# Moving the second pair's key rotation on GpSimd to the start of the kernel, and the last tokens' small copies to ScalarE

## The chip, the cores and the metric

The kernel runs on one NeuronCore of one Trainium2 chip. The metric is device time in microseconds (us) of one execution; lower is better. Five engines work side by side, each through its own instructions in order: TensorE (PE in the profile, with its weight loads as PEld), VectorE (DVE), ScalarE (ACT), GpSimd (POOL) and SyncE (SP), which here only issues transfers.

## The reference

Attention with rotary embedding over 2 batches of 8 heads (576 tokens, head size 64), then a dense feed-forward layer with softplus, then a mixture of eight experts of which each token takes one. Only the attention is touched here:

```python
def rotate(x):
    x1, x2 = (x[..., :half], x[..., half:])
    return np.concatenate([x1 * cos - x2 * sin, x1 * sin + x2 * cos], axis=-1)
q_rot, k_rot = (rotate(q), rotate(k))
scale = 1.0 / np.sqrt(D)
scores = scale * np.matmul(q_rot, k_rot.transpose(0, 1, 3, 2))
scores = scores - np.max(scores, axis=-1, keepdims=True)
attn = np.exp(scores)
attn = attn / (np.sum(attn, axis=-1, keepdims=True) + 1e-09)
return np.matmul(attn, v)
# then x = softplus(x @ w_in) @ w_out, and x = gate * relu(x @ w1[e]) @ w2[e] for each token's expert e
```

## The kernel before, in words

The 16 heads are worked on in 8 pairs (m = 0 to 7). Of each head's 576 tokens the first 512 lie as 128 partitions times 4, and the last 64 (the "tails") are handled apart. Numbers are kept exact by splitting each operand into a rounded high part and the rest, the low part.

For a pair, the raw keys and queries are rotated (`rotary`, L273: four elementwise instructions at L264, two multiplications of 128x512 by the cosines and sines, one subtraction and one addition of 128x256), turned by four TensorE transposes (`turn`, L311) and split: ScalarE copies the high part from PSUM (L341), VectorE subtracts it to give the low part (L359 for keys, L363 for queries). Both halves of the 128 partitions need copies, so `kqt` (L322) sends four transfers for a pair's keys (two after the high part, two after the low part) and six for its queries (four after the high part, two after the low part), all on SP's queue (L335, L365).

The first pair is on a path of its own (L1348 to L1365 and the steps for s up to 3): VectorE rotates its heads one after the other in 128x256 and 128x128 pieces (`first_rotary`, L410), `again` (L426) copies the rotated head beside itself, and the turns follow (`first_keys`, `first_queries`, `first_tails`). `first_tails` gives three steps: `more`, `second` (eight small copies for the first pair, L485) and `third` (seven small copies for the second pair, L495). `pcopy` (L67) is a copy on GpSimd, `acopy` (L70) one on ScalarE.

A loop over slots s then runs the scores: pair m = s // 9, block i = s % 9. A slot has the matmuls of one block (L526, `scores`), the row maximum on VectorE (L543) and the exponential on ScalarE (L544) one slot later; the PSUM banks of the scores alternate, so the matmuls of slot s wait for the exponential of slot s - 2. Work for coming pairs is put into the slots by hand: `later(n, f)` runs f at the end of the n-th slot from now, `tick` runs what is due. In slot 5 the second pair's queries are turned and split, in slot 6 its keys, and slot 9 is the second pair's first block. `warm(n)` adds n matmuls that feed nothing. The schedule is manual: each engine takes its instructions in program order.

Of the kernel before, what the change touches and what calls it, by code (L numbers as in the profile page):

```python
# [20 lines left out]
def kernel(  # L21
# [32 lines left out]
    NPR = NH // 2  # L54
# [12 lines left out]
    def pcopy(o, i):  # L67
        nc.gpsimd.tensor_scalar(out=o, in0=i, scalar1=1.0, scalar2=0.0, op0=ALU.mult, op1=ALU.add)  # L68

    def acopy(o, i):  # L70
        nc.scalar.activation(out=o, in_=i, func=ACTF.Copy)  # L71
# [145 lines left out]
    up, dn = slice(0, 64), slice(64, 128)  # L217
    xraw, rot, vst, kq, prob, stat, unit, xps, rsb, tls = ({} for _ in range(10))
# [54 lines left out]
    def rotary(m, nm, engs, ts=None):  # L273
        r = r_r[nm].next()
        rot[m, nm] = r
        out = r.rearrange("p (j h t d) -> p h j t d", j=4, h=2, t=2)
        return rotate(xraw.pop((m, nm)), False, *(ts or (r_t1.next(), r_t2.next())), out, engs)

    def rotary_tails(engs, c0=0):

        rot["t"] = x_tl
        x, t1, t2 = x_tl[:, c0:], r_t1.next()[:, c0:], r_t2.next()[:, c0:]
        return rotate(x, True, t1, t2, x.rearrange("p (g j t d) -> p g j t d", g=1, t=2, d=32), engs)
# [142 lines left out]
    def again(r, hs=slice(0, 2), copy=acopy):  # L426
        copy(r[:, :, hs, 1], r[:, :, hs, 0])
# [38 lines left out]
    def first_tails():  # L466

        tp = tbank()
        turn(tp, [rot["t0"][:, c, h].rearrange("p u d -> p (u d)") for c in range(2) for h in range(2)])
        hi, lo = r_u.bufs[2][:, 0:512], r_u.bufs[2][:, 512:1024]  # L470
        v = lambda a: a.rearrange("p (c h t s) -> p c h t s", c=2, h=2, t=2)
        hv, lv, tv = v(hi.bitcast(F32)), v(lo.bitcast(F32)), v(tp)
        st, w, _ = kq[0, "xk"]
        acopy(hi[:, 0:256], tp[:, 0:256])
        acopy(st[up, :, 576:640], tv[up, 0, :, 0])
        vsub(st[dn, :, 576:640], tv[dn, 0, :, 0], hv[dn, 0, :, 0])
        qs = tl_q[0][:, 0:512].rearrange("p (c h s) -> p c h s", c=2, h=2)
        ql = tl_ql[0][:, 0:256].rearrange("p (c h s) -> p c h s", c=2, h=2)

        def more():  # L480
            acopy(hi[:, 256:512], tp[:, 256:512])
            acopy(w[up, 576:640], tv[up, 0, 0, 0])
            later(1, lambda: vsub(lo, tp, hi.bitcast(F32)))

        def second():  # L485
            pcopy(w[dn, 576:640], hv[dn, 0, 1, 0])
            for h in range(2):
                pcopy(qs[:, :, h, 64 * h:64 * h + 64], hv[:, :, h, 1])
            pcopy(ql[up, :, 0], lv[up, :, 0, 1])
            pcopy(ql[dn, :, 1], lv[dn, :, 1, 1])  # L490
            pcopy(st[up, 1, 0:64], hv[up, 0, 1, 0])
            pcopy(st[dn, 1, 0:64], lv[dn, 0, 1, 0])
            pcopy(w[:, 0:64], hv[:, 0, 1, 0])

        def third():  # L495
            st, w, _ = kq[1, "xk"]
            for r, a in ((up, hv), (dn, lv)):
                pcopy(st[r, :, 576:640], a[r, 1, :, 0])
                pcopy(st[r, 1, 0:64], a[r, 1, 1, 0])
            pcopy(w[up, 576:640], hv[up, 1, 0, 0])  # L500
            pcopy(w[dn, 576:640], hv[dn, 1, 1, 0])
            pcopy(w[:, 0:64], hv[:, 1, 1, 0])

        return more, second, third

# [841 lines left out]
    vec, pool = nc.vector, nc.gpsimd  # L1347
# [6 lines left out]
    k_high()  # L1354
    q_high, q_low = first_queries(0)
    warm(4)
    again(rot["t0"])
    q_high()
    k_low()
    q_low()  # L1360
    t_more, t_second, t_third = first_tails()
    for f in first_rotary("xk", 1, vec, 4):
        f()
    again(rot[0, "xk"], slice(1, 2), pcopy)
    warm(3)  # L1365
    nc.vector.tensor_copy(tids, tokens.rearrange("p (t a) -> p t a", a=2))
    nc.scalar.dma_start(out=taut, in_=tau.rearrange("(a b) -> a b", a=1).to_broadcast([128, 1]))
# [4 lines left out]
    for s in range(NSL + 17):  # L1372
        m, i = divmod(s, 9)
        ma = m - 1 if 4 <= i <= 8 else m - 2
        add = None

        if hl:
            hl[0]()
        if ex:
            ex()  # L1380
        ending = 0 <= ma < NPR and i in (3, 8)
        if ending:
            add = fin(ma, i == 3)
        if hl:
            hl[1]()
        if hlt:
            hlt[0]()
        begin()
        ex = scores(m, i) if s < NSL else None
        if hlt:  # L1390
            hlt[1]()

        extra = None
        if i == (2 if m else 6) and m + 1 < NPR:
            extra = kqt(m + 1, "xk")
        if i == 5 and m + 1 < NPR:
            extra = kqt(m + 1, "xq")
        if i == 6 and 1 <= m <= NPR:
            extra = inv[2]()
        if i == 7 and m < NPR:  # L1400
            extra = tails(m)
        if i == 3 and 1 <= m <= NPR:
            extra = tails4(m - 1)
        if s == 8:
            extra = kqt_tails(0, 2)
        if s == 28:
            extra = kqt_tails(1)
        if s in (65, NSL + 7):
            extra = x_tails(0 if s == 65 else 1)
        if extra:  # L1410
            extra[0]()
        if add:
            add()
        if ending and i == 3:
            for n, f in enumerate(finish(ma)):
                later(n + 2, f)
        if extra:
            extra[1]()

        mt = m - 1 if i == 8 else None  # L1420
        if s >= NSL:
            mt = NPR - 1 if s == NSL + 5 else None
        hlt = av_tails(mt) if mt is not None and mt >= 0 else None
        if i and 0 <= ma < NPR:
            for u in AVS.get(i, ()):
                av(ma, u)

        mt, it = divmod(s - 10, 9)
        hl = transp(mt, UB[it]) if 0 <= mt < NPR else None
        if i == 0 and 0 <= ma < NPR:  # L1430
            for u in AVS.get(i, ()):
                av(ma, u)

        if s in UNPACK:
            unpack(True)
        if s >= FF:
            if s > FF and (s - FF) % 2 == 0:
                ffn1_act(*u_done)
                unpack(True)
            if (s - FF) % 2 == 0:  # L1440
                u_done = units.pop(0)
            ffn1_mm(*u_done, range(2 * ((s - FF) % 2), 2 * ((s - FF) % 2) + 2))
        if i == 5 and m < NPR:
            recip(m, slice(8, 9))
        if i == 0 and 1 <= m <= NPR:
            inv = inverse(m - 1)
            later(1, inv[0])
            later(2, inv[1])
        if i == 4 and m + 2 < NPR:
            for n, f in enumerate(rotary(m + 2, "xk", nc.gpsimd)):  # L1450
                later(n, f)
        if i == 8 and m + 2 < NPR:
            for n, f in enumerate(rotary(m + 2, "xq", nc.gpsimd)):
                later(n, f)
        if i == 8 and m + 3 < NPR:
            load(m + 3, "xk")
        if i == 4 and m and m + 2 < NPR:
            load(m + 2, "xq")
        if i == 1 and 1 <= m < NPR:
            load(m, "xv")  # L1460
        if i == 4 and m < NPR:
            for n, f in enumerate(vsplit(m)):
                later(n, f)
        if s == 5:
            for n, f in enumerate(vsplit_tails()):
                later(n, f)
        if s == 15:
            load_tails(1)

        if s == 21:  # L1470
            for f in rotary_tails(nc.gpsimd):
                f()
        if s == 46:
            for n, f in enumerate(vsplit_tails()):
                later(n, f)
        if s == 0:
            k_high, k_low = first_keys(1)
            k_high()
            t_more()
            later(1, t_second)  # L1480
        if s == 1:
            k_low()
            for f in first_rotary("xq", 1, vec, 6):
                f()
            again(rot[0, "xq"], slice(1, 2))
        if s == 2:
            for f in rotary(1, "xk", pool):
                f()
            q_high, q_low = first_queries(1)
            q_high()  # L1490
            for n, f in enumerate(rotary(1, "xq", nc.vector, (r_pp.bufs[5][:, 0:512], r_pp.bufs[5][:, 512:1024]))):
                later(min(n, 2), f)
            load(2, "xk")
            load(2, "xq")
        if s == 3:
            q_low()
        if s == 4:
            for f in rotary_tails(nc.gpsimd, 256):
                f()
        if s == 6:  # L1500
            t_third()
            for b in range(2):
                nc.gpsimd.memset(y_tl[b], 0.0)
        if s < 10:
            warm(2)
        tick()
        if s == NSL - 12:
            for _ in range(3):
                fetch()
# [339 lines left out]
```

## Time and profile before

| what | value |
|---|---|
| median of 3 runs | 532.79 us (531.74 to 533.05) |
| the profiled execution | 530.74 us |
| its span, first to last instruction | 529.0 us |
| TensorE matmuls busy | 505.5 us (96% of the span) |
| VectorE, ScalarE, GpSimd busy | 349.5, 312.7, 286.3 us |
| mean granted TensorE clock | 0.992 of full speed |

The rows count in microseconds from the span's start. In the timeline a row begins with start and duration; "x4" is four merged instructions, whose duration runs from the first start to the last end; the bracket gives idle time just before on that engine and what ended it. `fa` holds raw and rotated queries and keys, `g` scratch and probabilities, `rm` and `xd` the split operands, `pp` is PSUM.

### The profile page before, as it was taken

The numbers are of one execution on the slowest core, as the hardware profiler recorded it, in microseconds if no ns is written. First come the engines' busy times: TensorE is split into PE (matmuls) and PEld (weight loads), VectorE is DVE, ScalarE is ACT, GpSimd is POOL, SyncE is SP. The second block draws the span as 40 slices with busy tenths as digits, with TensorE's granted clock in tenths as the row PEclk, the third lists the DMA queues.
The fourth block names the chain that finished last, engine by engine and source line by source line (L and its number), as shares of the span: only waits on it lengthen the run. The fifth ranks groups of instructions, "written<-read, shape, count | busy, mean of one in ns | idle before, by whom it ended". The sixth has DMA issues, their size and how long they took to land. (4 is left out here: it accounts for less than half of the span.)

```text
span 529.0 us, 9306 instructions
## 1 busy us (share of the span) xinstructions
PE 505.5 (96%) x3184; PEld 449.8 (85%) x3184; DVE 349.5 (66%) x766; ACT 312.7 (59%) x662; POOL 286.3 (54%) x308
## 2 busy tenths in 40 slices
PE   7779999999989999999999999999999999999995
PEld 6578888889878989999998888888888989898794
DVE  7768888878899689999896222367647347156220
ACT  5569999999987666446966333345443255245321
POOL 1697889787436556654448445566775525300001
PEclk9889999999999999999999999999999999999999
DMA  7156656544643234444330000522221467600000
GB/s 177 39 136 173 163 125 163 150 115 114 152 148 91 80 120 151 156 144 159 124 114 2 14 28 21 145 69 86 61 105 43 150 257 241 212 10 21 20 6 34
DMA packets 45096, 57.09 MB, mean 108 GB/s; under 512 B 17112, under 2 KB 31448, under 8 KB 45040
## 3 DMA queue, kind: packets, MB, share of 16 engines
q1 hardware_dynamic: 41904, 48.76, 31.9%
q0 software_dynamic: 2704, 7.25, 4.0%
q8 instruction: 27, 0.44, 0.3%
q10 hardware_dynamic: 432, 0.41, 0.3%
q14 instruction: 29, 0.24, 0.1%
HBM read 40.17 MB, written 5.16 MB: 86 GB/s over the span
## 5 line engine op out<-in xcount | busy, mean ns | idle before, releaser
L803 PE MATMUL pp<-xb,rm 128*128 128x288 f32 x768 | 107.1, 298 | 1.8 <-POOL rm L68 1.0
L803 PEld LDWEIGHTS pp<-xb,rm 128*128 128x128 f32 x768 | 103.0, 189 | 4.4 <-DVE g L820 1.8
L845 PE MATMUL pp<-rm,parts 128*128 128x512 f32 x432 | 105.2, 397 | 0.0
L845 PEld LDWEIGHTS pp<-rm,parts 128*128 128x128 f32 x432 | 79.3, 188 | 15.8
L314 PE MATMUL pp<-ct,g 128*128 128x128 f32 x388 | 59.7, 276 | 5.0 <-ACT g L71 2.0
L74 DVE TENSOR_TENSOR rm<-pp,rm 128x512 fp32r<-128x512 f32 (+3 forms) x79 | 52.5, 669 | 13.9 <-ACT rm L71 13.0
L314 PEld LDWEIGHTS pp<-ct,g 128*128 128x128 f32 x388 | 47.3, 142 | 13.7 <-ACT g L71 2.4
L543 DVE TENSOR_REDUCE negm<-pp 128x1 f32<-128x576 f32 x72 | 53.9, 748 | 6.7 <-PE pp L526 6.6
L544 ACT ACTIVATE g<-pp,negm 128x576 f32<-128x576 f32 x72 | 53.2, 739 | 8.2 <-DVE negm L543 7.8
L81 POOL TENSOR_TENSOR rm<-fa,rm 128x512 fp32r<-128x512 f32 x34 | 46.2, 1359 | 12.1 <-ACT rm L71 7.1
L526 PE MATMUL pp<-rm 128*128 128x288 f32 x216 | 48.0, 331 | 4.7 <-DMA rm<-rm 2.7
L1079 PE MATMUL pp<-wa,parts 128*128 128x512 f32 x216 | 51.1, 393 | 0.0
L68 POOL TENSOR_SCALAR rm<-fa 128x512 fp32r<-128x512 f32 x27 | 18.3, 677 | 55.7 <-DVE fa L731 52.5
L71 ACT ACTIVATE rm<-pp 128x512 fp32r<-128x512 f32 (+3 forms) x73 | 42.1, 581 | 10.4 <-PE pp L314 7.9
L81 POOL TENSOR_TENSOR parts<-g,parts 128x512 fp32r<-128x512 f32 (+1 forms) x30 | 35.9, 1213 | 20.5 <-ACT parts L71 20.5
L1079 PEld LDWEIGHTS pp<-wa,parts 128*128 128x128 f32 x216 | 39.9, 188 | 8.0
L1222 PE MATMUL pp<-wa,wa 128*128 128x256 f32 x320 | 46.3, 283 | 0.0
L1222 PEld LDWEIGHTS pp<-wa,wa 128*128 128x128 f32 x320 | 42.9, 190 | 0.2
L526 PEld LDWEIGHTS pp<-rm 128*128 128x128 f32 x216 | 32.7, 194 | 10.1 <-ACT g L544 4.2
L612 PE MATMUL pp<-rm,rm 128*128 128x512 f32 x128 | 41.1, 413 | 0.0
L728 DVE SCALAR_TENSOR_TENSOR fa<-fa 128x512 int32<-128x512 int32 x32 | 39.5, 1235 | 0.8
L264 POOL TENSOR_TENSOR fa<-fa,g 128x512 f32<-128x512 f32 (+1 forms) x30 | 37.3, 1258 | 3.0 <-DMA fa<-in_q_dram 2.6
(219 smaller groups left out, 905.4 us busy)
## 6 DMA issues: line engine op xcount, KB each, us to landing
fa<-in_moe_w_in_dram SPq DMA_DIRECT2D x16, 512.0 KB, 3.8
fa<-in_moe_w_out_dram SPq DMA_DIRECT2D x16, 512.0 KB, 3.5
fa<-in_moe_w_dram SPq DMA_DIRECT2D x16, 512.0 KB, 6.0
rm<-rm SPq DMA_DIRECT2D x56, 128.0 KB, 2.4
ydram<-yst SPq DMA_DIRECT2D x9, 264.0 KB, 2.0
fa<-in_k_dram SPq DMA_DIRECT2D x8, 256.0 KB, 3.0
yst<-in_v_dram SPq DMA_DIRECT2D x8, 256.0 KB, 3.4
st<-in_moe_w_dram POOLq DMA_DIRECT2D x4, 512.0 KB, 9.7
```

The costliest lines, as they stand in the source:

```text
L71: nc.scalar.activation(out=o, in_=i, func=ACTF.Copy)
L74: nc.vector.tensor_tensor(out=o, in0=a, in1=b, op=ALU.subtract)
L81: nc.gpsimd.tensor_tensor(out=o, in0=a, in1=b, op=ALU.subtract)
L314: nc.tensor.matmul(out=bank[0:a.shape[1], i * 128:(i + 1) * 128], lhsT=a, rhs=ident, is_transpose=True, start=True, stop=True,)
L526: nc.tensor.matmul(out=ps[:, o:o + HS], lhsT=st, rhs=mv[:, k0 + o:k0 + o + HS], start=(x == 0), stop=(x == len(terms) - 1),)
L543: nc.vector.tensor_reduce(out=negm[:, col:col + 1], in_=ps, axis=AX.X, op=ALU.max, negate=True)
L544: return lambda: nc.scalar.activation(out=pr, in_=ps, func=ACTF.Exp, bias=negm[:, col:col + 1], accum_out=sums[:, col:col + 1])
L612: nc.tensor.matmul(out=pp[:, 7, :], lhsT=w, rhs=mv, start=(j == 0 and n == 0), stop=(j == 3 and n == len(terms) - 1))
L803: nc.tensor.matmul(out=hp[:, f, :], lhsT=wv[:, c * 128:(c + 1) * 128], rhs=xt[b][xi][:, c, f * HS:(f + 1) * HS], start=(n_mm == 0), stop=( ...
L845: nc.tensor.matmul(out=ybank(t), lhsT=ghl[gi][:, qd, c, :], rhs=wo[4 * qd + c][wi], start=(qd == 0 and c == 0 and gi == 0 and wi == 0), st ...
L1079: nc.tensor.matmul(out=pp[:, bank, :], lhsT=hid[a][i], rhs=wl[1][i], start=(i == 0 and a == 0 and wl is W.hi), stop=(i == K2F - 1 and a == 1),
L1222: nc.tensor.matmul(out=hp, lhsT=wl[0][2 * c + i // 4][:, i % 4 * 128:i % 4 * 128 + 128], rhs=mem[xi][c], start=(c == 0 and xi == "hi" and ...
```

## The change

Seven edits in the first slots. The copy of the rotated tails (`again(rot["t0"])`) goes from ScalarE to GpSimd, and the copy of the second head's rotated keys from GpSimd to ScalarE. The rotation of the second pair's keys on GpSimd goes from slot 2 to ahead of the loop, behind the tails' copy. The eight copies of `second` (end of slot 1) and the seven of `third` go from GpSimd to ScalarE, and `third` from slot 6 to slot 4. The turn, split and transfers of the second pair's keys go from slot 6 to slot 4. GpSimd's rotation of the remaining tails stays in slot 4.

```diff
         def second():
-            pcopy(w[dn, 576:640], hv[dn, 0, 1, 0])
+            acopy(w[dn, 576:640], hv[dn, 0, 1, 0])
             for h in range(2):
-                pcopy(qs[:, :, h, 64 * h:64 * h + 64], hv[:, :, h, 1])
-            pcopy(ql[up, :, 0], lv[up, :, 0, 1])
-            pcopy(ql[dn, :, 1], lv[dn, :, 1, 1])
-            pcopy(st[up, 1, 0:64], hv[up, 0, 1, 0])
-            pcopy(st[dn, 1, 0:64], lv[dn, 0, 1, 0])
-            pcopy(w[:, 0:64], hv[:, 0, 1, 0])
+                acopy(qs[:, :, h, 64 * h:64 * h + 64], hv[:, :, h, 1])
+            acopy(ql[up, :, 0], lv[up, :, 0, 1])
+            acopy(ql[dn, :, 1], lv[dn, :, 1, 1])
+            acopy(st[up, 1, 0:64], hv[up, 0, 1, 0])
+            acopy(st[dn, 1, 0:64], lv[dn, 0, 1, 0])
+            acopy(w[:, 0:64], hv[:, 0, 1, 0])
 
         def third():
             st, w, _ = kq[1, "xk"]
             for r, a in ((up, hv), (dn, lv)):
-                pcopy(st[r, :, 576:640], a[r, 1, :, 0])
-                pcopy(st[r, 1, 0:64], a[r, 1, 1, 0])
-            pcopy(w[up, 576:640], hv[up, 1, 0, 0])
-            pcopy(w[dn, 576:640], hv[dn, 1, 1, 0])
-            pcopy(w[:, 0:64], hv[:, 1, 1, 0])
+                acopy(st[r, :, 576:640], a[r, 1, :, 0])
+                acopy(st[r, 1, 0:64], a[r, 1, 1, 0])
+            acopy(w[up, 576:640], hv[up, 1, 0, 0])
+            acopy(w[dn, 576:640], hv[dn, 1, 1, 0])
+            acopy(w[:, 0:64], hv[:, 1, 1, 0])
...
     warm(4)
-    again(rot["t0"])
+    again(rot["t0"], copy=pcopy)
+    for f in rotary(1, "xk", pool):
+        f()
     q_high()
...
-    again(rot[0, "xk"], slice(1, 2), pcopy)
+    again(rot[0, "xk"], slice(1, 2))
...
-        if i == (2 if m else 6) and m + 1 < NPR:
+        if i == (2 if m else 4) and m + 1 < NPR:
             extra = kqt(m + 1, "xk")
...
         if s == 2:
-            for f in rotary(1, "xk", pool):
-                f()
             q_high, q_low = first_queries(1)
...
         if s == 4:
+            t_third()
             for f in rotary_tails(nc.gpsimd, 256):
                 f()
         if s == 6:
-            t_third()
             for b in range(2):
                 nc.gpsimd.memset(y_tl[b], 0.0)
```

## Rows read from the trace of the kernel before

**Rows 1.** The page: TensorE's busy tenths in 40 slices of 13.2 us.

```profile
PE   7779999999989999999999999999999999999995
```

**Rows 2.** Timeline of TensorE: start, us, line, operation, tiles, idle before.

```profile
13.00 0.66 PE L314 MATMUL pp<-ct,g 128*128 128x128 f32 x4 [0.96 <-POOL g L68]
19.55 1.60 PE L526 MATMUL pp<-rm 128*128 128x288 f32 x4
23.13 0.78 PE L526 MATMUL pp<-rm 128*128 128x288 f32 x4
25.93 0.66 PE L314 MATMUL pp<-ct,fa 128*128 128x128 f32 x4 [2.03 <-DVE fa L264]
34.79 0.51 PE L526 MATMUL pp<-rm 128*128 128x288 f32 x2 [2.73 <-DMA rm<-rm]
39.72 1.04 PE L526 MATMUL pp<-rm,xb 128*128 128x288 f32 x6
```

**Rows 3.** Windows: us, busy time (instructions) by engine, granted clock, DMA share, GB/s.

```profile
18.50:19.00 0.50, 0.50 (x4) 0.50 (x3) 0.50 (x2) 0.30 (x2) 0.42 (x2) 0.50 0.72 221
...
35.50:36.00 0.50, 0.50 (x5) 0.50 (x4) 0.40 (x1) 0.00 (x0) 0.50 (x2) 0.50 0.31 66
```

**Rows 4.** Timeline of SP's queue: start, time to issue, transfer.

```profile
27.25 2.46 SPq L335 DMA_DIRECT2D rm<-rm  x4
29.82 1.19 SPq L365 DMA_DIRECT2D xd<-fa  x2
31.11 2.46 SPq L335 DMA_DIRECT2D rm<-rm  x4
```

**Rows 5.** The page, part 6: issues, KB each, median us to landing.

```profile
rm<-rm SPq DMA_DIRECT2D x56, 128.0 KB, 2.4
...
fa<-in_k_dram SPq DMA_DIRECT2D x8, 256.0 KB, 3.0
```

**Rows 6.** Timeline of GpSimd, start to end of single instructions where not merged.

```profile
12.55 0.40 POOL L68 TENSOR_SCALAR g<-g 128x256 f32<-128x256 f32 x1 [9.64 <-DVE tids L1366]
12.93 0.61 POOL L68 TENSOR_SCALAR rm<-rm 64x512 fp32r<-64x512 f32 x1
20.33 2.51 POOL L264 TENSOR_TENSOR fa<-fa,g 128x512 f32<-128x512 f32 x2
22.92 1.13 POOL L264 TENSOR_TENSOR fa<-fa 128x256 f32<-128x256 f32 x1
24.01 0.72 POOL L264 TENSOR_TENSOR fa<-fa 128x256 f32<-128x256 f32 x1
25.56 0.91 POOL L264 TENSOR_TENSOR fa<-fa,g 128x256 f32<-128x256 f32 x1
```

**Rows 7.** Timeline of VectorE.

```profile
11.16 0.76 DVE L264 TENSOR_TENSOR g<-fa,g 128x256 f32<-128x256 f32 x2
11.96 0.49 DVE L264 TENSOR_TENSOR g<-g 128x128 f32<-128x128 f32 x2
21.26 0.76 DVE L543 TENSOR_REDUCE negm<-pp 128x1 f32<-128x576 f32 x1 [1.61 <-PE pp L526]
22.77 0.69 DVE L264 TENSOR_TENSOR g<-fa,g 128x512 f32<-128x512 f32 x1
24.17 0.84 DVE L264 TENSOR_TENSOR fa<-g 128x256 f32<-128x256 f32 x1
...
24.17 1.71 DVE L264 TENSOR_TENSOR fa<-g 128x256 f32<-128x256 f32 x2
```

**Rows 8.** Timeline of ScalarE.

```profile
10.54 0.26 ACT L71 ACTIVATE rm<-pp 64x128 fp32r<-64x128 f32 x1
17.67 0.42 ACT L71 ACTIVATE g<-g 128x256 f32<-128x256 f32 x1 [1.67 <-DVE g L264]
17.99 0.72 ACT L544 ACTIVATE g<-pp,negm 128x576 f32<-128x576 f32 x1
26.63 0.60 ACT L341 ACTIVATE rm<-pp 128x512 fp32r<-128x512 f32 x1 [1.51 <-PE pp L314]
```

## The prediction, made before the changed kernel was run

> **What bounds the kernel now.** I read the page first, then TensorE's timeline, then the queues that its long waits point to. The page shows TensorE busy in nine tenths or more of nearly every slice, and less in the first four and a few beyond [rows 1]. So from about 40 us on the kernel is as long as TensorE's work, and a change in the first slots counts by how much earlier or later the second pair starts (slot 9), plus what TensorE's clock loses around it.
>
> TensorE's timeline has two long stops there [rows 2]. At 25.93 it had waited 2.03 us for VectorE's rotation of the second pair's queries, at 34.79 it had waited 2.73 us for a transfer before slot 9. SP's queue tells which transfer: ten of one pair stand behind each other at about 0.61 us each, four after the queries' high part (from 27.25), two after their low part (29.82), then the four of the keys (31.11) [rows 4]. Slot 9 needs the first head only; of the keys' four that makes the third the last one needed, issued at 31.11 + 2 x 0.615 = 32.34, and with the median landing of 2.4 us [rows 5] it is there at 34.74, just when TensorE goes on. Had the keys gone ahead, the last need would have been the first low part of the queries: 29.82 + 2.4 = 32.2. That 2.5 us is what the change is after.
>
> The clock adds to it. At 35.5 the granted clock is 0.50, the 1.2 GHz level, after the idle stretch of 2.73 us; it is also 0.50 at 18.5 [rows 3], after a stretch with several stops, and there the four score matmuls of slot 3 take 1.60 us where slot 5's take 0.78 [rows 2].
>
> **The change part by part.**
>
> *The tails' copy* (128x256) goes from ScalarE, 0.42 us as for the same form [rows 8], to GpSimd, 0.40 [rows 6], and the second head's keys the other way: hundredths, taken as 0, bounds -0.1 and +0.1.
>
> *The early rotation.* GpSimd's copy starts about 9.0, so its two multiplications (2.51 us for both [rows 6]) run from 9.4 to 11.9, and VectorE's own rotation of the second head's keys starts at 11.16 and ends at 12.45 [rows 7]: they meet. The trace shows what a meeting costs, at 22.9 to 26.5, with GpSimd's old rotation beside VectorE's: GpSimd's 128x256 takes 1.13 in place of 0.72 [rows 6], and VectorE's pair 1.71 in place of 0.76 [rows 7]. One at a time explains the order: GpSimd ends at 24.01 + 0.72 = 24.73, VectorE 0.28 later (24.17 + 0.84 = 25.01), GpSimd's next some 0.59 after that (25.6), VectorE's second 0.28 later (25.88), GpSimd's last at 25.56 + 0.91 = 26.47, again 0.59 later. The same order from 11.93: VectorE 12.2, GpSimd 12.8, VectorE 13.1, GpSimd 13.7, then VectorE's two short ones, 13.95 and 14.2. VectorE is 1.75 us late. Bounds: 0 if they do not meet so, +2.3 if GpSimd's next instruction, the 64x512 copy of 0.61 [rows 6], also goes between. VectorE's rotation is on the path: the turn at 13.00 waits for its copy [rows 2], and behind it on VectorE stand slot 0's maximum and all that follows.
>
> The Trainium skill, SBUF — State Buffer, Terms (shared port pair), says that VectorE and GpSimd take a shared pair of ports exclusively for a whole instruction and the loser blocks. The rows agree for pairs of tensor operations; for GpSimd's copies beside a rotation, which the rule includes, VectorE would be 2.3 us late in place of 1.75 and the forecast 533.5; my rows show no meeting of that kind.
>
> *The query rotation of the second head* starts 1.28 us before its end at 17.63 (0.04 before the copy at 17.67 [rows 8]), so 16.35, now 18.1. GpSimd no longer waits: after its rotation and copy (14.3) come the remaining tails (half the size, estimated 2.4 us, to 16.7), then the third pair's key multiplications (their load is released at about 13.1 and lands in 3.0 [rows 5]), 16.7 to 19.2. VectorE meets the second and gets its first multiplication done at 19.5 in place of 18.5: +1.0, bounds 0 and 1.3 (one whole multiplication). ScalarE's copy then starts at 20.4, not 17.67.
>
> *The eight copies on ScalarE* come next in its queue, and behind them the exponential of slot 1, which followed the copy by 0.32 us (17.67 to 17.99 [rows 8]). A copy 128 wide takes 0.26 alone [rows 8]; successive ones overlap, as 0.32 of 0.42 shows. So 0.13 to 0.26 each, 1.0 to 2.1 us; I take 1.6 (five are 64 wide or wait for nothing but their turn). The exponential runs from 20.4 + 0.32 + 1.6 = 22.3 to 23.05, slot 3's scores wait for it and start about 23.2, not 19.55. Their maximum was at 21.26, 0.11 behind 19.55 + 1.60; now 23.2 + 0.78 + 0.11 = 24.1 at full clock, 24.9 at half: +2.85 or +3.65.
>
> *The keys' turn in slot 4* adds a turn (0.45 us of TensorE, beside other waits), and the keys' low part on VectorE (0.7) ahead of the last two instructions of the query rotation; these no longer meet GpSimd's, which takes 0.95 off. From slot 3's maximum to the end of the rotation it was 21.26 to 25.88, 4.62; now 4.4. The queries are ready at 28.5 or 29.3: +2.6 or +3.4.
>
> *The seven copies of `third`* with the keys' high part (0.6) come ahead of slot 4's exponential and the queries' high part on ScalarE, 0.9 to 1.8 us, where 1.51 us stood idle before 26.63 [rows 8]; taken as 0.3, bounds 0 and 0.9. If that idle time were gone, all of it would be on the path.
>
> *SP's queue.* The keys' four transfers are issued in 27 to 29.5, before the queries' high part (about 30), so they delay nothing; their landing is no longer the last. The queries' first low part comes at 32.2 + 2.6 + 0.3 = 35.1 or 32.2 + 3.4 + 0.3 = 35.9. Slot 6 loses its turn, copy and subtraction, which speeds nothing while slot 9 waits for that transfer.
>
> *After slot 9.* From 34.79 to slot 12's scores at 39.72 are 4.93 us [rows 2], most of it at half clock. At full clock the chain is slot 9's scores, maximum and exponential (0.78 + 0.76 + 0.72, with wake-ups 2.5) and then two slots' matmuls and turns, about 1.5: 4.0. With no long idle time before slot 9 the clock holds: -0.9, bounds 0 and -1.5.
>
> **Sum.** The clock fell before slot 3 already in the old order, and the stops ahead of it become longer, so I take the half clock there: slot 9 at 35.9, +1.1, less 0.9, gives +0.2. The span becomes 529.2, the execution 530.9 beside 530.74 of the profiled one. The median before is 2.05 above that, so the forecast is 532.79 + 0.2 = 533.0 us: the gain at SP's queue is paid for on VectorE and ScalarE.
>
> **The rivals.** *Faster: the two engines hardly meet.* If GpSimd's and VectorE's early instructions do not exclude each other, only ScalarE's copies remain: the exponential of slot 1 at 19.6, slot 3 at 20.5, its maximum between 21.3 and 22.2, so +0.1 to +0.9, the queries up to 0.7 late; slot 9 at 32.1 to 33.0 and -0.9: 2.7 to 3.6 us less, 529.2 to 530.1. For it speaks that a slot in between can fall by chance; against it every GpSimd time from 22.9 to 26.5 [rows 6]. A meeting of one rotation alone lies between.
>
> *Slower: the clock falls for longer.* TensorE now stops from 11.9 to 14.7 and from about 18.5 to 20.9, both about as long as the stop that the fall at 35.5 followed [rows 2, 3]. If slots 1 to 5 run at 1.2 GHz, two more scores and two turns on the path take twice as long (0.78 + 0.78 + 0.45 + 0.45, about 2.4). Slot 9 comes at 37.3 to 38.3, less 0.9: +1.6 to +2.6, 534.4 to 535.4. It decides as soon as slot 9 starts past 34.79 + 0.9 + 1.6 = 37.3. Against it: the turn at 25.93, right behind a stop of 2.03 us, takes 0.66 us as the one at 13.00 does [rows 2], so one such stop need not be enough.
>
> *Nothing moves*, because another transfer holds slot 9 where the keys did: that is inside my forecast.
>
> **How the numbers follow.** A measurement of this kernel tells about 0.3%, 1.6 us, from no change. My forecast 0.50 (its own range 531.9 to 534.3: slot 9 at 34.8 with the clock's 0.9, to slot 9 at 36.7 with 0.4 of it); the faster rival 0.26; the slower 0.24. Faster by over 0.3% means under 531.2, slower over 534.4. The range takes the better part of both rivals, 529.9 to 535.0, and leaves out about one in ten at either end.
>
> **What would show it.** Right: VectorE's key rotation ends near 14.2 with instructions of 0.7 to 1.0 us; the exponential of slot 1 starts past 22; the keys' transfers stand before the queries' on SP; slot 9 waits for a low part of the queries near 35 to 36; the granted clock is full after slot 9. Wrong: a key rotation ending by 12.6, or slot 9 before 33.5 (the faster rival), or half clock through slots 1 to 5 (the slower); and a difference that arises after 40 us would make all of this beside the point.

## The result, and the profile after

| | before | after |
|---|---|---|
| median (5 runs of each, same chip) | 531.74 us (529.96 to 533.05) | 536.72 us (536.31 to 538.51) |
| ratio, 95% interval | | 1.0100 (1.0077 to 1.0123) |
| profiled execution, its span | 530.74, 529.0 us | 538.51, 536.8 us |
| mean granted TensorE clock | 0.992 | 0.981 |

The change makes the kernel 5.0 us slower. The forecast was 533.0 us with a range up to 535.0: wrong, on the side of the slower rival and past that rival's own 535.4 as well. After's profiled execution is the longest of its five, 1.8 us over their median, and that of before lies 1.0 us under its median, so the rows of the two show 7.8 us of loss where the medians have 5.0.

The first place to look is where the two engines were said to meet. VectorE's timeline of after (start, us, line, operation, tiles, idle before), merged, and then the last instruction of the key rotation by itself:

```profile
11.22 0.29 DVE L74 TENSOR_TENSOR rm<-pp,rm 64x128 fp32r<-64x128 f32 x1 [0.46 <-ACT rm L71]
11.55 1.91 DVE L264 TENSOR_TENSOR g<-fa,g 128x256 f32<-128x256 f32 x2
13.49 2.69 DVE L264 TENSOR_TENSOR g<-g 128x128 f32<-128x128 f32 x2
...
14.11 2.07 DVE L264 TENSOR_TENSOR g<-g 128x128 f32<-128x128 f32 x1
```

GpSimd's timeline of after, same columns:

```profile
9.81 2.50 POOL L264 TENSOR_TENSOR fa<-fa,g 128x512 f32<-128x512 f32 x2
12.39 1.65 POOL L264 TENSOR_TENSOR fa<-fa 128x256 f32<-128x256 f32 x2
14.01 0.66 POOL L68 TENSOR_SCALAR rm<-rm 64x512 fp32r<-64x512 f32 x1
14.64 1.40 POOL L264 TENSOR_TENSOR fa<-fa,g 128x256 f32<-128x256 f32 x2
16.11 0.88 POOL L264 TENSOR_TENSOR fa<-fa 128x128 f32<-128x128 f32 x2
17.07 2.50 POOL L264 TENSOR_TENSOR fa<-fa,g 128x512 f32<-128x512 f32 x2
```

VectorE's four key instructions, 1.29 us before [rows 7], end at 16.18 instead of 12.45. The first three alternate with GpSimd's. The fourth stands from 14.11 to 16.18: in that time GpSimd runs its copy and both multiplications of the tails, at full speed (1.40 us for two multiplications of 128x256; one of that size next to VectorE took 0.91 [rows 6]), and only then does VectorE's 128x128 addition go through.

TensorE's timeline of after, the rows that answer to [rows 2]:

```profile
16.69 1.12 PE L314 MATMUL pp<-ct,g 128*128 128x128 f32 x4 [4.26 <-ACT g L71]
26.07 1.62 PE L526 MATMUL pp<-rm 128*128 128x288 f32 x4 [0.88 <-ACT g L544]
31.65 0.94 PE L526 MATMUL pp<-rm 128*128 128x288 f32 x4
33.23 0.66 PE L314 MATMUL pp<-ct,fa 128*128 128x128 f32 x4 [0.63 <-DVE fa L264]
39.15 0.51 PE L526 MATMUL pp<-rm 128*128 128x288 f32 x2
40.45 0.53 PE L526 MATMUL pp<-rm,xd 128*128 128x288 f32 x2 [0.79 <-DMA xd<-fa]
44.12 1.05 PE L526 MATMUL pp<-rm,xb 128*128 128x288 f32 x6
50.57 0.53 PE L526 MATMUL pp<-rm 128*128 128x288 f32 x2 [0.66 <-ACT g L544]
57.78 0.50 PE L526 MATMUL pp<-rm 128*128 128x288 f32 x2 [0.90 <-DMA rm<-fa]
```

The key turn comes at 16.69, not 13.00, after a stop of 4.26 us; slot 3 at 26.07, not 19.55; slot 5 at 31.65, not 23.13; slot 9 at 39.15 (its second half at 40.45), not 34.79 (35.13). Two stops at slots 15 and 18 (50.57, 57.78) are new (some of the expectations below call the first slot 14). One wait of TensorE for ScalarE that both traces have, 0.42 us before and 0.43 after, is below called **the mark**. The first of these rows is of before, the others are of after:

```profile
60.33 0.74 PE L612 MATMUL pp<-g 128*128 128x512 f32 x2 [0.42 <-ACT fa L71]
66.88 0.73 PE L612 MATMUL pp<-g 128*128 128x512 f32 x2 [0.43 <-ACT fa L71]
95.79 0.95 PE L526 MATMUL pp<-rm 128*128 128x288 f32 x4 [0.63 <-ACT rm L71]
```

The mark comes 6.55 us later; that is what was lost by then. Behind it the two traces run nearly in parallel: of the 1.3 us that the spans differ by beyond it, 0.8 come at one stop that only after has, at 95.79.

The clock, as windows of after (us, busy time and instructions by engine, granted clock, DMA share, GB/s):

```profile
14.00:16.00 2.00, 0.00 (x0) 0.00 (x0) 2.00 (x2) 0.00 (x0) 2.00 (x4) 0.74 0.44 131
16.00:32.00 16.00, 13.53 (x51) 11.49 (x52) 8.78 (x17) 8.75 (x26) 5.04 (x8) 0.50 0.06 17
32.00:34.00 2.00, 1.37 (x11) 1.14 (x11) 1.84 (x4) 1.95 (x8) 0.24 (x2) 1.00 0.49 114
```

It falls during the stop of 4.26 us and stays at 0.50, the 1.2 GHz level, for all of 16 to 32 us. Before, it was at 0.50 from about 18.4 to 21.8 and from 35.5 to 38.9 us, around the windows of [rows 3].

ScalarE's timeline of after, the copies:

```profile
22.75 0.42 ACT L71 ACTIVATE g<-g 128x256 f32<-128x256 f32 x1 [2.62 <-DVE g L264]
23.20 0.26 ACT L71 ACTIVATE rm<-rm 64x64 fp32r<-64x64 f32 x1
23.46 1.03 ACT L71 ACTIVATE xb<-rm 128x128 fp32r<-128x128 f32 x4
24.51 0.79 ACT L71 ACTIVATE rm<-rm 64x64 fp32r<-64x64 f32 x3
25.21 0.72 ACT L544 ACTIVATE g<-pp,negm 128x576 f32<-128x576 f32 x1
31.68 1.72 ACT L71 ACTIVATE rm<-rm 64x128 fp32r<-64x128 f32 x7
```

The eight put slot 1's exponential 2.46 us behind the copy at 22.75, where it was 0.32 [rows 8].

SP's queue in after:

```profile
31.81 5.51 SPq L335 DMA_DIRECT2D rm<-rm  x8
37.42 1.19 SPq L365 DMA_DIRECT2D xd<-fa  x2
45.56 0.54 SPq L233 DMA_DIRECT2D yst<-in_v_dram  x1
54.67 1.18 SPq L365 DMA_DIRECT2D rm<-fa  x2
```

This is the part that the change was for, and it works: the keys' four transfers stand before the queries', and the last that slot 9 waits for is the low part of the queries.

### The profile page after: what moved, and what is told of

The parts are those of the page before. It is cut to its first block, busy times and chain, and to the rows that moved or that the text cites. A ratio compares the mean times of both kernels' runs of the same rounds, so it can differ in the third digit from the quotient of the medians.

```text
span 536.8 us, 9302 instructions
## 1 busy us (share of the span) xinstructions
PE 509.0 (95%) x3184; PEld 452.0 (84%) x3184; DVE 348.6 (65%) x766; ACT 317.3 (59%) x677; POOL 283.0 (53%) x293
## 5 line engine op out<-in xcount | busy, mean ns | idle before, releaser
L81 POOL TENSOR_TENSOR parts<-g,parts 128x512 fp32r<-128x512 f32 (+1 forms) x30 | 36.0, 1217 | 19.6 <-ACT parts L71 19.5
```

The costliest lines, as they stand in the source:

```text
L81: nc.gpsimd.tensor_tensor(out=o, in0=a, in1=b, op=ALU.subtract)
```

## The experiments

Each ratio is to runs of the kernel before on the same chip, with its 95% interval. The chips differ between runs, and on them the median of the kernel before lay between 531.16 and 531.74 us. "Mark" is that of the run's one profiled execution, and a single execution carries about 1 us of chance: the kernel of run 12 and the kernel before are the same up to slot 8, and yet slot 8 comes at 31.37 and 30.38, with the half clock lasting from about 17.7 to 24.5 in one and from 18.4 to 21.8 in the other.

**1. Only the rotation and the turn.** All fifteen copies stay on GpSimd, as before (the edit is against after):

```diff
-            acopy(w[dn, 576:640], hv[dn, 0, 1, 0])
+            pcopy(w[dn, 576:640], hv[dn, 0, 1, 0])
...
         if s == 4:
-            t_third()
         if s == 6:
+            t_third()
```

> The changed kernel with the fifteen small copies back on GpSimd (the eight at the end of slot 1, the seven in slot 6); the early rotation, the swapped copies and the keys' turn in slot 4 stay. Theory A (GpSimd's early instructions hold up VectorE's rotation of the second head's keys, and the clock falls behind that): the eight copies now wait on GpSimd for ScalarE, so nothing but the rotation and one copy can stand in VectorE's way; its key rotation ends at 14.5 to 15 in place of 12.45, still 2 us late, slot 9 near 36, and the time is 2 to 4 us above the kernel before. Theory B (ScalarE's queue: the copies ahead of the exponentials cost most of it): without them slot 9 comes at about 33 and the time is 1 to 3 us below the kernel before.

533.24 us, ratio 1.0022 (1.0007 to 1.0036), mark 63.04: somewhat less than the 2 to 4 us expected. VectorE's timeline in this run, and what GpSimd does behind its rotation:

```profile
11.75 1.90 DVE L264 TENSOR_TENSOR g<-fa,g 128x256 f32<-128x256 f32 x2
13.68 1.31 DVE L264 TENSOR_TENSOR g<-g 128x128 f32<-128x128 f32 x2
...
14.20 0.98 POOL L68 TENSOR_SCALAR rm<-rm 64x512 fp32r<-64x512 f32 x2
18.27 0.56 POOL L68 TENSOR_SCALAR xb<-rm 128x128 fp32r<-128x128 f32 x2 [3.09 <-ACT rm L71]
```

The key rotation ends at 14.99, 1.95 us late when the start (0.59 later) is taken off. Here GpSimd stands 3.09 us before a small copy that waits for ScalarE's output, and its tails stand behind that copy: it cannot run on into VectorE. The small copies had been a **hold** on GpSimd.

**2. Only the copies.** Before with the fifteen on ScalarE (the edit of the change's first two pieces, `third` staying in slot 6).

> The kernel before with the fifteen small copies on ScalarE and nothing else changed (the seven still in slot 6). Theory A: VectorE's key rotation ends at 12.5 as before; slot 3 starts some 1.5 us later behind the eight copies, slot 9 still waits for the keys' transfers behind the queries', so plus 0.5 to 2 us. Theory B: plus 4 to 5 us, as the whole change.

533.94 us, 1.0050 (1.0033 to 1.0066), mark 62.90: this half alone costs no less than the other half alone, and more than the 0.5 to 2 us expected. GpSimd, no longer held, reaches the second pair's rotation at 13.54, though the code still has it in slot 2, and its next instructions meet VectorE's query rotation:

```profile
16.11 1.59 POOL L264 TENSOR_TENSOR fa<-fa 128x256 f32<-128x256 f32 x2
17.78 1.52 POOL L264 TENSOR_TENSOR fa<-fa,g 128x256 f32<-128x256 f32 x2
...
16.37 1.61 DVE L264 TENSOR_TENSOR g<-fa,g 128x256 f32<-128x256 f32 x2
18.02 1.43 DVE L264 TENSOR_TENSOR g<-g 128x128 f32<-128x128 f32 x2
```

1.61 and 1.43 in place of 0.76 and 0.49, then the eight copies: slot 3 at 22.78.

**3. The rotation behind the copy of the keys.** After, with GpSimd taking that copy again and the rotation queued behind it, so that it cannot meet the key rotation:

```diff
-    for f in rotary(1, "xk", pool):
-        f()
     q_high()
...
-    again(rot[0, "xk"], slice(1, 2))
+    again(rot[0, "xk"], slice(1, 2), pcopy)
+    for f in rotary(1, "xk", pool):
+        f()
```

> The changed kernel, but GpSimd takes the copy of the second head's rotated keys again, and the second pair's rotation stands behind that copy, so it starts when VectorE's key rotation has ended. Theory A: the key rotation ends at 12.5, the turn comes at 13.1 in place of 16.7, the first half-clock stretch is short, slot 9 comes at 34 to 36 and at least 3 of the 5 us are gone; what is left comes from the query rotation meeting GpSimd and from ScalarE's copies. Theory B: slot 3 stays behind the copies, and no more than 1 to 2 us are gone.

533.62 us, 1.0043 (1.0029 to 1.0057), mark 63.09. The key rotation ends at 12.75, undisturbed, and the query rotation takes the meeting in its place (1.69 and 1.43, ends at 19.80). It recovers about 3 us of the 5, not all.

**4. The clock alone.** After, with matmuls that feed nothing in two stops:

```diff
         if s == 0:
+            warm(14)
             k_high, k_low = first_keys(1)
...
         if s == 2:
+            warm(8)
             q_high, q_low = first_queries(1)
```

> The changed kernel with 14 more filler matmuls ahead of the turn of the second head's keys and 8 ahead of the turn of its queries, which TensorE runs while it would stand still (about 3.5 and 2 us at full clock). If the clock's fall at 15.5 to 32 is the larger part of the loss, the granted clock stays 1.00 through slots 1 to 5 and 2 to 3 of the 5 us are gone. If the chain through VectorE and ScalarE is what costs, the clock holds and less than 1 us is gone.

533.52 us, 1.0036 (1.0023 to 1.0050), mark 63.09. The key rotation is as late as in after (its last pair 13.49 2.70), but the clock stays up:

```profile
16.00:32.00 16.00, 12.10 (x86) 10.47 (x86) 11.12 (x21) 12.28 (x38) 7.06 (x12) 1.00 0.20 50
```

Slot 8 comes at 34.19, not 37.73. So the half clock of 16 to 32 us carries about 3.2 us of the loss (536.72 less 533.52).

**5. The key rotation out of the way, copies on GpSimd.** Run 1 with the order of run 3: of the change, only the earlier rotation, the turn in slot 4 and the tails' copy on GpSimd are left.

> The run with the rotation behind the key copy, and with the fifteen small copies back on GpSimd (the seven in slot 6), so that only the rotation and the keys' turn have moved. Theory A (the two engines' meetings): the key rotation ends at 12.5; the query rotation, which starts near 16.4, meets the end of GpSimd's rotation and its copies and ends at 18.5 to 19 in place of 17.6; slot 9 at 33.5 to 35, the time within 1 us of the kernel before or up to 1 us below. Theory B (ScalarE's copies): slot 9 at 32 to 33, 2 us below.

531.35 us, 0.9997 (0.9980 to 1.0014), mark 60.53. The key rotation ends at 12.43, the query rotation at 18.54 (17.63 before), slot 9's second half starts at 34.44.

**6. One more copy off that path.** Run 5 with the 64x512 copy of the first head's keys on ScalarE ahead of the loop:

```diff
-            pcopy(w[up], kq[0, "xk"][0][up, 0, 64:576].bitcast(F32))
...
+    acopy(kq[0, "xk"][1][up, 64:576], kq[0, "xk"][0][up, 0, 64:576].bitcast(F32))
```

> The run before it, and the 64x512 copy of the first head's keys taken by ScalarE ahead of the loop, where it stands idle, so that GpSimd's rotation is over by 17.0 and its next work waits for the low part of the tails. Theory A: the query rotation ends at 18.2 to 18.5, half a microsecond before the run before it, and the time is 0.3 to 1 us below that run. Theory B: no difference between the two runs.

530.56 us, 0.9979 (0.9965 to 0.9993), mark 60.42: a little faster than before by the medians, while the mark is that of before (60.33). Of all that slot 9 gains little arrives: behind it TensorE stops where before it did not.

```profile
34.26 0.53 PE L525 MATMUL pp<-rm,xd 128*128 128x288 f32 x2 [0.77 <-DMA xd<-fa]
44.17 0.53 PE L525 MATMUL pp<-rm 128*128 128x288 f32 x2 [0.38 <-ACT g L543]
51.26 0.50 PE L525 MATMUL pp<-rm 128*128 128x288 f32 x2 [0.80 <-DMA rm<-rm]
52.06 0.53 PE L525 MATMUL pp<-rm 128*128 128x288 f32 x2 [0.30 <-DMA rm<-fa]
...
42.49 0.42 ACT L71 ACTIVATE rm<-yst 128x256 fp32r<-128x256 f32 x1 [0.98 <-DMA yst<-in_v_dram]
```

**7. The hold by itself.** After, with one of the eight copies left on GpSimd, ahead of its tails:

```diff
-            acopy(ql[dn, :, 1], lv[dn, :, 1, 1])
+            pcopy(ql[dn, :, 1], lv[dn, :, 1, 1])
```

> The changed kernel with one of the eight copies of slot 1 left on GpSimd, where it has to wait for VectorE's low part of the tails, so that the rotation of the tails and the third pair's multiplications cannot follow at once. ScalarE keeps the other fourteen. Theory A: VectorE's last key instruction is no longer passed over by the tails' multiplications, the key rotation ends at 15.0 in place of 16.2, and about 1.2 us come back before the clock, 1 to 2 us in the time. Theory B: no more than 0.3 us, one copy's worth.

534.53 us, 1.0044 (1.0029 to 1.0059), mark 63.95. One 64-partition copy, which does nothing for VectorE but keep GpSimd waiting, takes 2.2 us off the changed kernel; that ScalarE has one copy of about 0.26 us less to do cannot be all of it. The last pair of the key rotation takes 1.31, as in run 1, not 2.69:

```profile
13.29 1.31 DVE L264 TENSOR_TENSOR g<-g 128x128 f32<-128x128 f32 x2
```

**8. The clock in the kernel before.** Filler matmuls in its stops (3, 4, 7 and 9 of them, the last ahead of slot 9).

> The kernel before with filler matmuls in its long stops: 3 ahead of the key turn of slot 0, 4 ahead of the query turn of slot 2, 7 in slot 5 and 9 ahead of slot 9. Theory C (the clock alone): the granted clock stays 1.00 at 18.5 to 21.7 and at 35.5 to 38.6, slot 12 comes 0.9 us sooner after slot 9, and the time is 1 to 2 us below the kernel before. Theories A and B say nothing on it; if the clock cost nothing there, no difference.

531.18 us, 0.9987 (0.9974 to 1.0000), mark 60.98. The clock is full up to the mark (mean 0.999), slot 9 to slot 12 takes 3.91 us in place of 4.93, and nothing of it reaches the mark, so that the 1 to 2 us expected do not come: slot 15 now stops 1.06 us for ScalarE, which had waited 1.76 us for the values' load, and slot 18 0.47 us for a transfer.

**9. Run 6 with filler matmuls.**

> The run with GpSimd's rotation behind the key copy and the 64x512 copy on ScalarE, with filler matmuls in TensorE's stops: 3 ahead of the key turn of slot 0, 6 ahead of the query turn of slot 2, 4 in slot 5. If the clock's fall at 18.6 to 25.5 still costs in this order, the granted clock stays 1.00, slot 3's maximum comes 0.8 us sooner, slot 9 at 33 to 33.5 in place of 34.3, and the time is 1 to 2 us below the kernel before. If the second pair's start is not what sets the end any more (the third pair's transfers do), slot 9 comes sooner but the time stays within 0.5 us of the run without filler.

531.12 us, 0.9998 (0.9978 to 1.0017), mark 61.72. No gain. Its profiled execution began some 0.9 us late, with a wait for the constants, its clock still fell from about 28.3 to 31.7 us, and slot 15 stops 2.46 us behind ScalarE, which waited 3.12 us for the values' load. It shows no further gain from the clock, and no more can be read from it.

**10. Run 6 with the keys' turn back in slot 6.**

```diff
-        if i == (2 if m else 4) and m + 1 < NPR:
+        if i == (2 if m else 6) and m + 1 < NPR:
```

> The same run without filler, and with the turn, split and transfers of the second pair's keys back in slot 6, behind the queries'. It tells what the order on SP's queue is worth by itself. By the reading of the kernel before, slot 9 then waits for the keys' third transfer again, near 35.5 to 36 in place of 34.3, and 1 to 2 us are lost. If the order on that queue is worth nothing, no difference.

531.68 us, 1.0006 (0.9989 to 1.0023), mark 61.47. Slot 9 waits 2.73 us for the keys' transfer, as before, and its second half starts at 36.37, 2.1 us later than in run 6; the mark is 1.05 later. So the new order on SP's queue is worth 2.1 us at slot 9 and, by medians from two chips (531.68 and 530.56), about 1 us at the end.

**11 to 14. Where slot 9's gain goes.** In the trace of before SP issues one transfer after the other from 27 to 54 us. In run 6 it pauses 1.0 us, from 32.45 to 33.44, ahead of the small transfers of slot 8, and from there issues without a pause to 55 us. Both new stops wait for it: slot 15 by way of the values' load, which stands behind eight small transfers and a load of keys, slot 18 for the third pair's transfers. So three raw loads go from SP's queue to ScalarE's: in run 11 in the kernel of run 6, in run 12 in the kernel before, in run 13 in the changed kernel. Run 14 is run 11 with the first of the three (keys, slot 8) left on SP.

```diff
-            load(m + 3, "xk")
+            load(m + 3, "xk", nc.scalar if s < 18 else nc.sync)
-            load(m + 2, "xq")
+            load(m + 2, "xq", nc.scalar if s < 18 else nc.sync)
-            load(m, "xv")
+            load(m, "xv", nc.scalar if s < 18 else nc.sync)
```

> The version of the run e6 (early rotation behind the key copy, no copies moved to ScalarE but the 64x512 one, turn in slot 4), with three raw loads (third further pair's keys in slot 8, second pair's values in slot 10, third pair's queries in slot 13) issued on ScalarE's queue in place of SP's. Theory (what slot 9 gains is given back because SP issues without a pause from about 26 to 54 us, so that the values' load and the third pair's transfers stay where they were): the values' load is issued about 37 in place of 39.4, ScalarE's wait of 0.98 for it at 42.5 is gone, the waits of TensorE at slots 14 (0.38) and 18 (0.80 and 0.30) shrink or go, the marker past 60 us comes 1.0 to 1.5 us earlier, 529.2 to 529.8 us. Rival (the end is set by work of the engines in slots 10 to 18, not by SP's queue): the waits move elsewhere and the time stays at that of e6, 530.6 +- 0.5.

> The kernel before with only those three loads moved from SP's queue to ScalarE's. Theory: in the order of before slot 9 itself waits for a transfer issued ahead of these loads, and stays at 34.8; behind it the waits at slots 14 and 18 shrink, so 0.3 to 1.2 us less, 530.1 to 531.0. If SP's queue behind slot 9 is no bound there: no difference, 531.3 +- 0.5. Against e11 it tells what the earlier slot 9 is worth once the queue behind it is freed: the theory wants e11 to gain more over e6 than e12 over the kernel before, or the two to differ by 1 us or more.

> The changed kernel with only the three raw loads (keys in slot 8, values in slot 10, queries in slot 13) issued on ScalarE's queue in place of SP's. Its early part, with slot 9 near 39.2 and 40.5, stays. Theory (behind slot 9 the changed kernel loses part of what it had caught up because SP's queue has no pause from there to the third pair's transfers): the waits of 0.66 at slot 14 and 0.90 and 0.23 at slot 18 go, from the second half of slot 9 to the marker past 60 us it takes 24 to 25 us in place of 26.4, 535.0 to 535.7 us in place of 536.7. Rival (the end is set elsewhere): 536.7 +- 0.5, with the waits at other places.

> The version with the early rotation behind the key copy and the turn in slot 4 (530.56 before), with the values' load of slot 10 and the queries' load of slot 13 on ScalarE's queue, and the keys' load of slot 8 still on SP's, so that it does not run beside the transfers that slot 9 waits for. Theory as above, and that in the run with three loads moved the median (530.29) hid part of the gain that its one profile (528.1) showed because the early keys' load disturbs slot 9 in some executions: 529.0 to 529.8. If the early load does no harm and the queue behind slot 9 is no bound: 530.3 to 530.6.

| run | median | ratio | second half of slot 9 | mark |
|---|---|---|---|---|
| 11 | 530.29 | 0.9975 (0.9960 to 0.9991) | 33.81 | 57.90 |
| 12 | 532.18 | 0.9998 (0.9979 to 1.0017) | 37.60 | 62.18 |
| 13 | 535.56 | 1.0077 (1.0051 to 1.0103) | 40.40 | 65.96 |
| 14 | 529.28 | 0.9952 (0.9933 to 0.9972) | 34.04 | 57.85 |

Run 14 is the fastest kernel of the study, 0.48% under the kernel before. TensorE, ScalarE's queue and ScalarE in it:

```profile
34.04 0.53 PE L525 MATMUL pp<-rm,xd 128*128 128x288 f32 x2 [0.77 <-DMA xd<-fa]
57.85 0.73 PE L611 MATMUL pp<-g 128*128 128x512 f32 x2 [0.44 <-ACT fa L71]
...
35.46 0.41 ACTq L233 DMA_DIRECT2D yst<-in_v_dram  x1
41.00 0.41 ACT L71 ACTIVATE rm<-yst 128x256 fp32r<-128x256 f32 x1
```

The values' load goes out at 35.46 (39.38 in run 6), ScalarE's wait of 0.98 us and the stops at slots 15 and 18 are gone, and from slot 9's second half to the mark it takes 23.81 us, not 26.16. The rival, that the engines' own work sets the end there, falls. The Trainium skill, DMA: Bandwidth & Descriptors, Issuing engines are not separate DMA queues, says that starting transfers from several engines saves only the time that it takes to start them, usually small beside the transfer itself. In run 6 that time was 0.54 and 1.24 us for these two, and taking them off SP is worth 1.3 us of the kernel (530.56 to 529.28, on two chips; the two intervals just touch): less than the two together. Here it lay on the path; the values' load itself goes out 3.9 us earlier, since on SP it stood behind the transfers named above. In run 13 the stop at slot 15 is gone as well, but slot 18 still stops, 1.64 us; the median is 1.2 us lower, less certain, since the two intervals overlap.

Run 12 shows the other side: the keys' load, issued early on another queue, runs beside the transfers that slot 9 waits for. The DMA view of 32 to 38 us (KB each, median us to landing):

```profile
rm<-rm SPq DMA_DIRECT2D x4, 128.0 KB, 3.8
fa<-in_k_dram ACTq DMA_DIRECT2D x1, 256.0 KB, 3.3
```

3.8 us in place of 2.4 [rows 5], and slot 9 stops 4.21 us, where it was 2.73 [rows 2]; the other 1.0 us of its lateness was there at slot 8 already and has nothing to do with the load. The 0.3 to 1.2 us expected of run 12 did not come. Whether the load is also why the median of run 11 lies 1 us above that of run 14, and above the 529.2 to 529.8 expected, though their profiled executions have the same mark, is open: the intervals overlap, and in run 11's profile slot 9 shows no harm.

## Why the prediction was wrong, point by point

**What bounds the kernel** was read rightly: most of the loss is made ahead of slot 9, and the order of SP's queue changed as described. "A difference that arises after 40 us" did not decide it, but it has its share of the 7.8 us between the two profiled executions: the second half of slot 9 is 5.3 us late (40.45 for 35.13), the mark 6.55, the end 7.8. The 0.2 us that the forecast added stood on a median of three runs, 532.79; five runs put it at 531.74, which is not what made it wrong.

**The early rotation, +1.75, bounds 0 and +2.3: the step that failed.** Measured +3.3 (16.18 less 12.45, less the later start of 0.39). The mechanism is right and for three instructions the order too. The step took it that each GpSimd instruction lets a waiting one of VectorE's through, and that the tails, which the next paragraph of the same sum puts right behind GpSimd's copy, are no part of this meeting. They are: copy, multiplication, multiplication, 0.66 + 1.40 us, and VectorE's addition has waited for all three. With the hold in place (runs 1 and 7, last pair 1.31) the same meeting costs 1.95 us, near the forecast; there GpSimd's 64x512 copy does go between, as in the bound of +2.3 (in run 1 the copy ends at 14.85, the addition at 14.99). The Trainium skill, SBUF — State Buffer, Who interferes with whom, says that issue order decides who blocks. The alternation agrees with that; the addition at 14.11, passed by two instructions that started at 14.64 and 15.32, does not.

What was not weighed at all is that the moved copies held GpSimd back. The prediction followed GpSimd's queue as work that starts earlier, not as work that nothing keeps away from VectorE any more; run 2 shows it in the other order too.

**The query rotation, +1.0.** It did not happen in after: VectorE is so late there that GpSimd's multiplications are over by 19.6. In runs 2 and 3 it did, with +1.8 and +1.9.

**Eight copies, 1.6, bounds 1.0 and 2.1.** Measured 2.1 (2.46 less 0.32), the upper bound: they run at 0.26 us each. **Seven copies, +0.3:** 1.72 us, ahead of slot 4's exponential. Together with the keys' high part they put about 0.4 us on the path: the queries' turn ends at 33.89, but their high part has to wait for that exponential and starts at 34.32; before, it followed the turn by 0.04.

**The keys' turn in slot 4**, 4.4 us from slot 3's maximum to the end of the query rotation: 5.37 in after (27.80 to 33.17), where slot 4's matmuls and the turn ran at half clock, and 4.26 in run 4 (25.76 to 30.02) with the clock up. The term held only for the full clock.

**The clock.** "I take the half clock there" was right for slot 3 and too little for slots 1 to 5. The rival had that stretch, priced at +1.6 to +2.6 in all, with the point of decision at slot 9 past 37.3; slot 9 came at 39.15. Of its signs "half clock through slots 1 to 5" is what came. It was put aside because one stop of 2.03 us had left the clock up [rows 2]; the stop of after is 4.26 us, because of the failed step. Run 4 prices the stretch at 3.2 us.

**After slot 9, -0.9.** Two things failed. In after there is nothing to give back before slot 12 (39.15 to 44.12 is 4.97, as before), since slot 9's own second half waits. And where the clock does return, in run 8, its 1.0 us ends at slot 15, in the wait for the values' load. The sum treated slot 9 as the yardstick of the end; SP's queue behind it is the next bound, which was not looked at because in the trace of before it hides behind the late slot 9.

**The sum.** By steps of medians: run 5 (earlier rotation held, turn in slot 4) 0.0; the rotation ahead of the key copy 1.9 (run 1 less run 5); ScalarE's copies 1.3 (run 7 less run 1); GpSimd's tails running on 2.2 (after less run 7); 5.4 together beside 5.0 measured. By the ratios the steps are 1.3, 1.2 and 3.0. The medians come from different chips, and each step has an uncertainty of about 1 us, so their order of size is not settled, and the smallest, ScalarE's copies, is barely told from zero. The steps also hold for this order only: taken first, in run 2, the copies cost 2.3 us (533.94 less 531.64). The clock's 3.2 is contained in these, not added to them.

## What to carry to other kernels

An instruction that waits can be doing a job: before a small wait is taken off a helper engine, look at what stands behind it in that queue and whom that will run into. Where two engines shut each other out, put the helper's long work behind an instruction that already waits for the critical engine to be done (run 3's order), rather than trust in taking turns. And a gain at one block is worth what the next queue lets through: by their ratios run 6 gained about 1 us, and run 14, where two loads had left SP's queue, 2.5.

## What the runs showed of the hardware

A VectorE addition of 128x128 that takes 0.28 us alone (12.16 in before) took 2.07 us, passed over by one GpSimd copy and two multiplications; in other places (12.39 to 14.0) the two engines took turns. What decides between turns and being passed over is not shown.

VectorE's subtractions with one operand in PSUM were not held: the 64x512 one takes 0.69 us beside GpSimd's subtraction in run 5 as it does in before with GpSimd idle (at 8.97). It is VectorE instructions with both operands in SBUF that were held. Both engines' rows in run 5:

```profile
15.62 0.69 DVE L74 TENSOR_TENSOR rm<-pp,rm 64x512 fp32r<-64x512 f32 x1
15.48 1.41 POOL L264 TENSOR_TENSOR fa<-fa 128x256 f32<-128x256 f32 x2
```

Small ScalarE copies in a row cost 0.25 to 0.26 us each, from 64x64 to 128x128: eight took 2.10 us, seven 1.72.

The same instructions do not always meet the same clock: with equal code up to slot 8, the first stretch at 0.50 ended at about 21.8 us in before and at 24.5 in run 12.
